# Combine weights transposed four token tiles at a time, and the output product on four groups of 32 rows in three passes

## The chip, the cores and the metric

The kernel runs on one core of a Trainium2 chip. Its five engines are TensorE (matmuls, with weight loads as instructions of their own), VectorE, ScalarE, GpSimd and SyncE, which here only issues transfers. The metric is the device time of one execution in microseconds; lower is better.

## What is computed

Three stages in float32: a linear attention with a normalisation over the head dimension, a feed-forward layer with the gate h * cos(h), and a soft mixture of experts. The change lies in the last one. There are 4608 tokens of 512 channels, 8 experts with 4 slots each (32 slots), and a hidden size of 1024 per expert.

```python
logits = x @ phi                                  # 4608 x 32
d = exp(logits - logits.max(0)); d /= d.sum(0) + 1e-9
slot_input = (d.T @ x).reshape(8, 4, 512)
for e in range(8):
    slot_out[e] = maximum(slot_input[e] @ w1[e], 0) @ w2[e]
c = exp(logits - logits.max(1)); c /= c.sum(1) + 1e-9
out = c @ slot_out.reshape(32, 512)               # 4608 x 512
```

The last line is the output product: for each token the 32 combine weights `c` times the 32 slot outputs.

## The kernel before

**Body.** The tokens go through in ten blocks (eight of 512 tokens, two of 256). For each block the first matrix of the feed-forward layer is applied in 16 column groups (`main`, line 389, three matmuls in place of one, because each operand is split in a high and a low part of the reduced type fp32r), the cosine gate runs on ScalarE and VectorE, and logits and slot inputs are accumulated. Steps for the next block (attention, loads, transposes) are woven into this loop at slots given by the table PLAN; each engine runs its own instructions in the order in which they are written down, since the schedule is manual. The body ends near 610 us.

**Tail.** `tail` (line 743) holds everything that the change touches but a small setup. The 32 slots are handled as two sets G of four experts. `first_layer(G)` and `relu(G)` make the hidden activations, `h_T` transposes them, `second_layer(G, h)` (line 795) multiplies with the second matrix for one half h of the 512 channels. It has eight steps r; in a step four matmuls write to four groups of 32 output partitions, one for each expert, and each float32 matmul is two instructions. Its argument `then` names other work to be put behind a step r on TensorE. Its result is copied to `so[G]` by ScalarE (line 805).

**Combine weights.** `c_softmax` leaves the weights as `tok[0]`, 128 tokens by 36 tiles by 32 slots. The output product needs them transposed, slots on partitions, and split in a high and a low part. `c_split(j)` (line 716) makes, on GpSimd, for four token tiles the three blocks high, low, high of 32 columns each; `c_T(j)` (line 727) transposes each of these four 96-column tiles with a matmul against the identity, and ScalarE or VectorE copies the 512 columns out of PSUM (line 736). There are nine j, so 36 transposes.

**Output product.** `select(h)` (line 807) gathers the 32 slot rows of a half from the two `so` by a matmul with a constant 0/1 matrix `sel`, three copies of them on 96 partitions: high, high and low part. `part_out(h, u)` (line 818) then makes output tile u (six for each half: three token groups n by two blocks k of 128 channels): three matmuls of 96 rows by 512 tokens, so that high*high, high*low and low*high are summed within one matmul. Each result is copied from PSUM to `ot` by VectorE or ScalarE in turn, and SyncE writes the 768 KB tile out (line 831; the very last tile in three pieces, line 829).

**Banks.** PSUM has the pools `ps_m` (three banks, tags "h"), `ps_l` (one) and `ps_a` (four, through `at_bank`). `part_out` uses the three of `ps_m`.

**Loads.** The expert matrices are read by `fill`, in order of use, into any buffer that has come free, on the queue of SyncE. The lists `early`, `mid` and `last` (lines 1029 to 1032) are issued within the tail; an issue waits until the former content of its buffer was read, and everything behind it on that queue waits too. `sel_init` (line 1035) builds the selection matrix on GpSimd during block 3.

Of the kernel before, what the change touches and what calls it, by code (L numbers as in the profile page):

```python
# [8 lines left out]
F32 = mybir.dt.float32  # L9
F32R = mybir.dt.float32r  # L10
I32 = mybir.dt.int32
AF = mybir.ActivationFunctionType
ALU = mybir.AluOpType
# [20 lines left out]
    start=(  # L34
# [3 lines left out]
    ),  # L38
# [18 lines left out]
    lo=(1, 1, 0, 0),  # L57
# [5 lines left out]
TB = 512  # L63
# [4 lines left out]
NT = sum(TT)  # L68
# [4 lines left out]
def tile_linear_attention__ffn_cos__soft_moe(  # L73
# [14 lines left out]
    nc = tc.nc  # L88
    B, H, D = kv.shape[0], 8, 64
    NF, KD = w_in.shape[0], w_in.shape[2]  # L90
    NS = phi.shape[2]

    const = ctx.enter_context(tc.tile_pool(name="const", bufs=1))
    w_p = ctx.enter_context(tc.tile_pool(name="w", bufs=1))
    x_p = ctx.enter_context(tc.tile_pool(name="x", bufs=1))
# [8 lines left out]
    one_p = ctx.enter_context(tc.tile_pool(name="one", bufs=1))  # L104
    ps_m = ctx.enter_context(tc.tile_pool(name="ps_m", bufs=PLAN["pm"], space=bass.MemoryType.PSUM))
    ps_l = ctx.enter_context(tc.tile_pool(name="ps_l", bufs=1, space=bass.MemoryType.PSUM))
    ps_a = ctx.enter_context(tc.tile_pool(name="ps_a", bufs=PLAN["pa"], space=bass.MemoryType.PSUM))

    ident = const.tile([128, 128], F32, name="ident")
    rep32 = const.tile([128, NS], F32, name="rep32")  # L110
    rep = const.tile([128, 4, NS], F32, name="rep")
    sel = const.tile([128, 2, 3, NS], F32, name="sel")
    mhalf = const.tile([128, H], F32, name="mhalf")
    hpi = const.tile([128, 1], F32, name="hpi")
    gn = const.tile([128, 1], F32, name="gn")
    phi_sb = const.tile([128, KD, NS], F32, name="phi_sb")
# [14 lines left out]
    tok = []  # L131

    def at_bank(name):
        return ps_a.tile([128, 512], F32, tag="at", name=name)

    def copy_on(e, out, in_):
        (nc.vector.tensor_copy if e else nc.scalar.copy)(out=out, in_=in_)
# [573 lines left out]
        nc.vector.reciprocal(out=st[:, 1], in_=st[:, 1])  # L711
        nc.vector.tensor_tensor(out=l_tok, in0=l_tok, in1=st[:, 1].to_broadcast([128, n, NS]), op=ALU.mult)

    cs_t, cT_t = [], []

    def c_split(j):
        if j == 0:
            w = x_p.tile([128, 9, 4, 3 * NS], F32, tag="x1", name="cs")
            cs_t.extend(w[:, x] for x in range(9))
        cs = cs_t[j]  # L720
        c = tok[0][:, 4 * j:4 * j + 4, :]
        hi, lo, hi2 = (cs[:, :, i * NS:(i + 1) * NS] for i in range(3))
        nc.gpsimd.tensor_copy(out=hi.bitcast(F32R), in_=c)
        nc.gpsimd.tensor_tensor(out=lo.bitcast(F32R), in0=c, in1=hi, op=ALU.subtract)
        nc.gpsimd.tensor_copy(out=hi2.bitcast(F32R), in_=c)

    def c_T(j):
        if j % 4 == 0:
            n = min(9 - j, 4)
            pool, tag = ((x_p, "x00"), (x_p, "x01"), (w_p, "w9"))[j // 4]  # L730
            x = pool.tile([128, n, 512], F32R, tag=tag, name="cT")
            cT_t.extend(x[:, i] for i in range(n))
        ps = at_bank("cT")
        for t in range(4):
            nc.tensor.transpose(ps[0:96, t * 128:(t + 1) * 128], cs_t[j][:, t, :], ident)
        copy_on(j % 2 == 0, cT_t[j][0:96], ps[0:96])

    def warm(n):
        ps = at_bank("warm")
# [3 lines left out]
    def tail():  # L743
        nc.vector.tensor_scalar(out=s_run, in0=s_run, scalar1=1e-9, scalar2=None, op0=ALU.add)
        nc.vector.reciprocal(out=s_run, in_=s_run)
        ps = si_t.pop()
# [4 lines left out]
        for i in range(2):  # L751
            cc = slice(128 * i, 128 * i + 128)
            nc.vector.tensor_scalar(out=flat[:, cc], in0=ps[:, cc], scalar1=s_run, scalar2=None, op0=ALU.mult)
            cc = slice(128 * i + 256, 128 * i + 384)
# [3 lines left out]
        ps = at_bank("sT").rearrange("p (k s) -> p k s", s=128)  # L758
        for kk in (0, 2, 1, 3):
            nc.tensor.matmul(out=ps[:, kk, 0:NS], lhsT=part[:, kk], rhs=rep32, start=True, stop=True)  # L760
        for G in range(2):
            nc.vector.tensor_copy(out=Z[G][:, :, :, 0:4],
                                  in_=ps[:, :, 16 * G:16 * G + 16].rearrange("p k (i t) -> p k i t", t=4))
# [26 lines left out]
            (nc.scalar.copy if u else nc.vector.tensor_copy)(out=dst, in_=ps)  # L790

        so = [a_p.tile([128, 512], F32, tag="a", name="so") for _ in range(2)]
        st_all = one_p.tile([128, 2, 256], F32R, tag="ls", name="st")

        def second_layer(G, h, then={}):
            ps = (at_bank("eo") if h == 2 else ps_m.tile([128, 512], F32, tag="h", name="eo"))[:, 0:256]
            c = (h - 1) * 256
            for r in range(8):
                for i in range(4):
                    w = GR.pop((4 * G + i, 1, h, r))  # L800
                    nc.tensor.matmul(out=ps[32 * i:32 * i + 32, :], lhsT=hT[G][0][:, r, 32 * i:32 * i + 32],  # L801
                                     rhs=w, start=(r == 0), stop=(r == 7))
                for fn, *a in then.get(r, ()):
                    fn(*a)
            nc.scalar.copy(out=so[G][:, c:c + 256], in_=ps)

        def select(h):
            cc = slice(256 * (h - 1), 256 * h)
            ps = at_bank("sel")[:, 0:256]
            for G in range(2):  # L810
                nc.tensor.matmul(out=ps[0:96], lhsT=sel[:, G].rearrange("p c s -> p (c s)"), rhs=so[G][:, cc],
                                 start=(G == 0), stop=(G == 1))
            st = st_all[:, h - 1]
            nc.scalar.activation(out=st[0:96], in_=ps[0:96], func=AF.Copy)
            nc.vector.tensor_tensor(out=st[64:96], in0=ps[64:96], in1=st[64:96].bitcast(F32), op=ALU.subtract)
            return st

        def part_out(h, u):
            st, ots = half[h]
            ot = ots[u]  # L820
            n, k = divmod(u, 2)
            for v in range(3):
                ps = ps_m.tile([128, 512], F32, tag="h", name="fo")
                nc.tensor.matmul(out=ps, lhsT=st[0:96, 128 * k:128 * k + 128], rhs=cT_t[3 * n + v][0:96],  # L824
                                 start=True, stop=True)
                cc = slice(512 * v, 512 * v + 512)
                copy_on((3 * u + v) % 2, ot[:, cc], ps)
                if (h, u) == (2, 5):
                    nc.sync.dma_start(out=out[3, 2, :, cc], in_=ot[:, cc])
            if (h, u) != (2, 5):  # L830
                nc.sync.dma_start(out=out[2 * h - 2 + k, n], in_=ot)

        def two(pool, tag):
            t = pool.tile([128, 2, 1536], F32, tag=tag, name="ot")
            return [t[:, 0], t[:, 1]]
# [6 lines left out]
        relu(1)  # L842
        for fn, *args in mid:
            fn(*args)
        for j in range(9):
            c_split(j)
        second_layer(0, 1, {2: [(h_T, 1, 0)], 4: [(h_T, 1, 1)], 6: [(c_T, 0)]})
        for fn, *args in last:
            fn(*args)
        assert not todo  # L850
        second_layer(1, 1, {0: [(c_T, 1)], 4: [(c_T, 2)]})
        half = {}

        def first_half():
            half[1] = (select(1), two(g_p, "g1") + [gt_p.tile([128, 1536], F32, tag=f"gt{i}", name="ot") for i in (1, 0)]
                       + two(g_p, "g0"))

        second_layer(0, 2, {0: [(first_half,)], 1: [(c_T, 3)], 2: [(part_out, 1, 0)], 4: [(part_out, 1, 1)],
                            5: [(c_T, 4)], 6: [(c_T, 5)]})
        second_layer(1, 2, {0: [(part_out, 1, 2)], 2: [(part_out, 1, 3)], 3: [(c_T, 6)], 4: [(c_T, 7)], 5: [(c_T, 8)],  # L860
                            7: [(part_out, 1, 4)]})
        half[2] = (select(2), [t_p.tile([128, 1536], F32, tag="T2", name="ot")] + two(g_p, "g1")
                   + [gt_p.tile([128, 1536], F32, tag="gt1", name="ot")] + two(g_p, "g0"))
        part_out(1, 5)
# [95 lines left out]
    for b in range(1, B):  # L960
        p, i = divmod(b, 2)
        n, sl = b - 2, PLAN["kv"]
        if b < 4:
            n, sl = PLAN["K"][b - 1]
# [3 lines left out]
    for j in range(1, NB):  # L968
        n = min(j - 1, SMALL - 1)
# [5 lines left out]
        for t in range(TT[j]):  # L975
            i = T0[j] + t + 3
# [25 lines left out]
    for u in range(NF):  # L1002
        n, i = 3 + u // 4, u % 4
        a, f = PLAN["nt"][i]
# [22 lines left out]
    for n in range(8, 15):  # L1027
        ld_at(9, max(n + 1, 10), fill, w_p, f"w{n}", 2)
    early = [(fill_kv, i) for i in range(4)] + [(fill, rem_p, "vr", 1), (fill, rem_p, "kr", 2), (fill, t_p, "T2", 4)] + [
        (fill, q_p, f"q{i}", 1) for i in range(3)] + [(fill, const, "kvA", 2)]  # L1030
    mid = [(fill, w_p, f"w{n}", 2) for n in range(10, 13)]
    last = [(fill, w_p, f"w{n}", 2) for n in range(13, 16)]
    Z = []

    def sel_init():
        nc.gpsimd.memset(sel, 0.0)
        id4 = ident.rearrange("p (i t) -> p i t", t=32)[:, :, 0:4]
        for G in range(2):
            for c in range(3):
                nc.gpsimd.tensor_copy(  # L1040
                    out=sel[:, G, c, 16 * G:16 * G + 16].rearrange("p (i t) -> p i t", t=4), in_=id4)

    late(3, 2, sel_init)

    def z_init():
# [44 lines left out]
    with tc.manual_schedule():  # L1090
# [34 lines left out]
        for j, f in [(j, f) for j in range(SMALL, NB) for f in range(0, NF, 2)]:  # L1125
            if (j, f) == (NB - 1, NF - 2):
                for i in range(2):
                    ps = ps_m.tile([128, 512], F32, tag="h", name="h")[:, 0:256]
# [10 lines left out]
            ps = ps_m.tile([128, 512], F32, tag="h", name="h")  # L1139
# [22 lines left out]
        fill(t_p, "T1", 4)  # L1162
        fill(t_p, "T0", 4)
        tail()
        assert not any((side, post, fin, loads))

# [55 lines left out]
```

## Time and profile before

| | |
|---|---|
| time, median of 3 runs | 685.14 us (684.58 to 687.48) |
| the profiled execution | 686.2 us, of which its span is 684.2 us |
| TensorE matmuls busy | 659.3 us, 96% of the span |
| VectorE, ScalarE, GpSimd busy | 497.9, 332.4, 217.4 us (73%, 49%, 32%) |
| granted TensorE clock, mean | 0.987 of full speed |
| read and written over the span | 91.29 MB and 13.63 MB |

The span runs from the first instruction of the profiled execution to its last; the time of the execution holds 2.0 us more around it. A share of busy time is a mean over the whole span, and the tail's 75 us are a ninth of it, so the rows below are nearly all from the tail.

### The profile page before, as it was taken

The page shows a single profiled execution, that of the slowest core. Times are in us where ns is not written, and L with a number is a line of the kernel's source. Part 1 is how long each engine was busy: PE and PEld are TensorE (multiplying, and loading weights), DVE is VectorE, ACT ScalarE, POOL GpSimd, SP SyncE. Part 2 cuts the span into 40 slices and gives each one's busy share as a digit, 9 for nine tenths or more (in the row PEclk, how much of TensorE's full clock was granted, in tenths as well). Part 3 has the DMA queues.
Part 4 walks back from the last instruction along what each step waited for, and adds up shares of the span by engine and source line. Part 5 has one row for each costly group of instructions (what it writes and reads, how often), then busy time and mean ns, then how long its engine had stood idle before and what let it go on. Part 6 is the DMA issues. An engine that isn't in the chain of part 4 may idle for free.

```text
span 684.2 us, 12526 instructions
## 1 busy us (share of the span) xinstructions
PE 659.3 (96%) x4580; PEld 479.3 (70%) x4580; DVE 497.9 (73%) x895; ACT 332.4 (49%) x589; POOL 217.4 (32%) x320
## 2 busy tenths in 40 slices
PE   7989999999999999999999999999999999999994
PEld 6767877776667776776777677767767779863542
DVE  3899989966677778887887888778877756444143
ACT  3576767645345445436455444544545344641243
POOL 3351111320364434521633344154335423002200
PEclk9999999999999999999999999999999999999995
DMA  9944564111374627783767378486534498999968
GB/s 334 350 167 175 181 217 167 60 34 62 92 187 139 185 63 219 210 212 111 192 191 192 106 200 233 102 226 175 131 105 96 84 319 249 362 394 408 399 247 322
DMA packets 72892, 135.11 MB, mean 197 GB/s; under 512 B 11008, under 2 KB 38784, under 8 KB 72448
## 3 DMA queue, kind: packets, MB, share of 16 engines
q1 hardware_dynamic: 65664, 119.63, 53.9%
q0 software_dynamic: 7168, 14.69, 9.2%
q8 instruction: 36, 0.59, 0.3%
q14 instruction: 24, 0.20, 0.1%
HBM read 91.29 MB, written 13.63 MB: 153 GB/s over the span
## 4 chain that ended last, share of the span: by engine, by line
PE 68%; DVE 12%; ACT 6%; SPq 5%; DMA 5%; issue 3%; POOL 0%; DVEq 0%; ACTq 0%
PE h L389 39%; PE ab L622 5%; SPq L511 4%; PE ops L202 3%; DMA g<-tr 3%; PE l L523 3%; PE eo L801 2%; DVE gT L451 2%; PE eh L771 2%; DVE tmp L408 2%; PE fo L824 2%; PE tr L492 2%; PE xTps L239 2%; ACT tmp L412 2%; PE kvps L183 2%
## 5 line engine op out<-in xcount | busy, mean ns | idle before, releaser
L389 PE MATMUL h<-xt,w 128*128 128x512 f32 (+1 forms) x1920 | 421.0, 374 | 4.1 <-DVE xt L252 1.7
L389 PEld LDWEIGHTS h<-xt,w 128*128 128x128 f32 x1920 | 329.5, 189 | 87.1 <-issue 12.7
L412 ACT ACTIVATE tmp<-tmp,hpi 128x512 f32<-128x512 f32 (+1 forms) x145 | 104.3, 721 | 173.4 <-DVE tmp L408 173.2
L511 POOL DMA_DIRECT2D g<-tr x224 | 123.8, 555 | 101.1 <-DVE tr L470 49.0
L451 DVE TENSOR_TENSOR gT<-tmp,h 128x512 f32<-128x512 f32 x130 | 89.2, 686 | 70.6 <-ACT tmp L412 70.5
L214 POOL TENSOR_TENSOR ri<-ss,mhalf 128x8 f32<-128x8 f32 x36 | 59.7, 1662 | 202.1 <-DVE ss L212 197.2
L408 DVE SCALAR_TENSOR_TENSOR tmp<-h,tmp 128x512 f32<-128x512 f32 (+1 forms) x145 | 97.1, 673 | 21.0 <-ACT tmp L405 20.2
L405 ACT ACTIVATE tmp<-h 128x512 int32<-128x512 f32 (+1 forms) x145 | 85.3, 588 | 48.4 <-PE h L389 48.1
L470 DVE STREAM_TRANSPOSE tr<-gT 128x512 f32<-128x512 f32 x103 | 73.2, 711 | 5.9 <-DMA g<-tr 1.5
L325 POOL TENSOR_TENSOR w<-st_m,w 128x512 fp32r<-128x512 f32 x16 | 21.4, 1340 | 68.6 <-ACT w L320 65.3
L202 PE MATMUL ops<-kvA,q 128*128 128x128 f32 (+1 forms) x320 | 38.3, 278 | 0.1
L243 ACT ACTIVATE xt<-xTps,gn 128x512 fp32r<-128x512 f32 x36 | 24.3, 684 | 27.4 <-PE xTps L239 27.4
L202 PEld LDWEIGHTS ops<-kvA,q 128*128 128x128 f32 (+1 forms) x320 | 34.4, 180 | 3.2 <-issue 2.3
L622 PE MATMUL ab<-g,d 128*32 128x512 f32 x256 | 32.3, 593 | 0.0
L523 PE MATMUL l<-gT,wp 128*32 128x512 f32 (+1 forms) x248 | 30.9, 556 | 0.0
L209 ACT ACTIVATE sq<-ops 128x512 f32<-128x512 f32 x32 | 19.1, 596 | 22.0 <-PE ops L202 21.8
L252 DVE SCALAR_TENSOR_TENSOR xt<-xTps,gn,xt 128x512 fp32r<-128x512 f32 x36 | 26.1, 730 | 4.9 <-ACT xt L243 4.6
L211 DVE TENSOR_REDUCE ss<-sq 128x8 f32<-128x512 f32 x32 | 21.6, 676 | 7.1 <-ACT sq L209 6.7
L183 PEld LDWEIGHTS kvps<-kv 128*64 128x64 f32 x448 | 15.4, 137 | 11.6 <-issue 7.6
L239 PE MATMUL xTps<-ident,sq 128*128 128x128 f32 x128 | 19.7, 277 | 3.4 <-DVE sq L221 3.4
L622 PEld LDWEIGHTS ab<-g,d 128*32 128x32 f32 x256 | 9.4, 110 | 19.3 <-issue 16.8
L221 DVE TENSOR_TENSOR sq<-ops,ri 128x512 f32<-128x512 f32 x32 | 21.5, 676 | 1.2 <-POOL ri L214 1.2
(185 smaller groups left out, 634.9 us busy)
## 6 DMA issues: line engine op xcount, KB each, us to landing
kv<-in_kv SPq DMA_DIRECT2D x28, 512.0 KB, 5.4
g<-tr SPq DMA_DIRECT2D x224, 64.0 KB, 3.6
g<-tr POOLq DMA_DIRECT2D x224, 64.0 KB, 3.7
ew<-in_w2h SPq DMA_DIRECT2D x19, 512.0 KB, 10.0
q<-in_qT SPq DMA_DIRECT2D x36, 256.0 KB, 5.9
out<-ot SPq DMA_DIRECT2D x11, 768.0 KB, 4.4
rw<-in_w_in SPq DMA_DIRECT2D x16, 512.0 KB, 4.6
nat<-in_w_out SPq DMA_DIRECT2D x16, 512.0 KB, 4.0
```

Of the source, the lines that this page charges most:

```text
L202: nc.tensor.matmul(out=ps[p0:p0 + n, pr * 128:(pr + 1) * 128], lhsT=q_t[j, t][:, pr, p0:p0 + n], rhs=kvbd[b % 2][:, pr, :], start=True, st ...
L214: nc.gpsimd.tensor_tensor(out=ri[:, :, 0], in0=ss, in1=mhalf, op=ALU.pow)
L239: nc.tensor.transpose(ps[:, kk * 128:(kk + 1) * 128], xs[:, kk * 128:(kk + 1) * 128], ident)
L389: nc.tensor.matmul(out=ps, lhsT=w[:, a, kk, :], rhs=x[b][:, kk, :], start=(n == 0), stop=(n == 3 * KD - 1))
L405: nc.scalar.activation(out=t.bitcast(I32), in_=ps, func=AF.Copy, bias=0.25, scale=INV_2PI)
L408: nc.vector.scalar_tensor_tensor(out=t, in0=ps, scalar=INV_2PI, in1=t.bitcast(I32), op0=ALU.mult, op1=ALU.subtract)
L412: nc.scalar.activation(out=t, in_=t, func=AF.Sin, bias=hpi, scale=TWO_PI)
L451: nc.vector.tensor_tensor(out=g, in0=fr, in1=h_t.pop((j, f)), op=ALU.mult)
L470: nc.vector.transpose(out=tr_t[j, q][:, :, i, :], in_=gT_t[j, n * q + i].rearrange("p (b t) -> p b t", t=32))
L511: (nc.gpsimd if b % 2 else nc.sync).dma_start(out=dst[32 * b:32 * b + 32, :, x, a:a + n, :].rearrange("p t f i -> p t (f i)"), in_=src[32 ...
L523: nc.tensor.matmul(out=l_t[j][32 * o:32 * o + 32, :], lhsT=wp[:, f, :], rhs=gT_t.pop((j, f)), start=(c == 0), stop=(c == (2 if j == NB - 1 ...
L622: nc.tensor.matmul(out=ps[32 * c:32 * c + 32, :], lhsT=d[:, t, :], rhs=gs[c // 2][t][:, (c % 2) * 512:(c % 2) * 512 + 512], start=(t == 0) ...
```

## The change

1. `c_split` goes. `c_T(n)` (three calls) transposes four token tiles of 32 slots at once, 128 columns by 128 tokens, three such transposes into one bank of 384 columns. ScalarE copies the bank as the high part, VectorE subtracts to get the low part. Slot s of tile 4i + g then lies on partition 32g + s. Nine transposes stand in place of 36, all behind step 6 of `second_layer(0, 1)`.
2. `select` makes four copies of the 32 rows on 128 partitions, with two matrices `sel` and `phi_sb` (the buffer of phi, which is free by then). ScalarE copies the high part, VectorE subtracts for the low part, all 128 partitions each.
3. `part_out` uses the four groups of 32 partitions as four separate products of 384 tokens: three passes (high*high, high*low, low*high), each of four matmuls into four banks. Four copies of 384 columns empty them. The three odd tiles of the second half use the four banks of `ps_a`, the others those of `ps_m` and `ps_l`. The last tile goes out in four pieces.
4. The transposed weights lie in the buffer x1 in place of x00, x01 and w9, so the last loads go to w9 and x00 in place of w13 to w15. The places at which the first half's output tiles are woven into `second_layer` move.
5. The host reorders the output by the new token order.

```diff
-    sel = const.tile([128, 2, 3, NS], F32, name="sel")
+    sel = const.tile([128, 4, NS], F32, name="sel")
-    def c_split(j):
...
-        hi, lo, hi2 = (cs[:, :, i * NS:(i + 1) * NS] for i in range(3))
-        nc.gpsimd.tensor_copy(out=hi.bitcast(F32R), in_=c)
-        nc.gpsimd.tensor_tensor(out=lo.bitcast(F32R), in0=c, in1=hi, op=ALU.subtract)
-        nc.gpsimd.tensor_copy(out=hi2.bitcast(F32R), in_=c)
-    def c_T(j):
...
-        ps = at_bank("cT")
-        for t in range(4):
-            nc.tensor.transpose(ps[0:96, t * 128:(t + 1) * 128], cs_t[j][:, t, :], ident)
-        copy_on(j % 2 == 0, cT_t[j][0:96], ps[0:96])
+    def c_T(n):
+        if not cT_t:
+            x = x_p.tile([128, 4096], F32R, tag="x1", name="cT")
+            m = NT * NS
+            cT_t.extend(x[:, m * i:m * i + m] for i in range(2))
+            cT_t.append(x[:, 2 * m:2 * m + 1024].rearrange("p (h a c) -> p h a c", h=2, a=2))
+        ps = at_bank("cT")[:, 0:384]
+        for t in range(3):
+            i = 4 * (3 * n + t)
+            nc.tensor.transpose(ps[:, t * 128:(t + 1) * 128], tok[0][:, i:i + 4, :].rearrange("p t s -> p (t s)"), ident)
+        hi, lo = (x[:, 384 * n:384 * n + 384] for x in cT_t[0:2])
+        nc.scalar.copy(out=hi, in_=ps)
+        nc.vector.tensor_tensor(out=lo, in0=ps, in1=hi.bitcast(F32), op=ALU.subtract)
...
         def select(h):
-            for G in range(2):
-                nc.tensor.matmul(out=ps[0:96], lhsT=sel[:, G].rearrange("p c s -> p (c s)"), rhs=so[G][:, cc],
+            for G, t in enumerate((sel, phi_sb)):
+                nc.tensor.matmul(out=ps, lhsT=t.rearrange("p c s -> p (c s)"), rhs=so[G][:, cc],
...
-            nc.scalar.activation(out=st[0:96], in_=ps[0:96], func=AF.Copy)
-            nc.vector.tensor_tensor(out=st[64:96], in0=ps[64:96], in1=st[64:96].bitcast(F32), op=ALU.subtract)
+            hi, lo = (cT_t[2][:, h - 1, a] for a in range(2))
+            nc.scalar.copy(out=hi, in_=ps)
+            nc.vector.tensor_tensor(out=lo, in0=ps, in1=hi.bitcast(F32), op=ALU.subtract)
         def part_out(h, u):
-            for v in range(3):
-                ps = ps_m.tile([128, 512], F32, tag="h", name="fo")
-                nc.tensor.matmul(out=ps, lhsT=st[0:96, 128 * k:128 * k + 128], rhs=cT_t[3 * n + v][0:96],
-                                 start=True, stop=True)
-                cc = slice(512 * v, 512 * v + 512)
-                copy_on((3 * u + v) % 2, ot[:, cc], ps)
+            if h == 2 and u % 2:
+                ps = [at_bank("fo") for _ in range(4)]
+            else:
+                ps = [ps_m.tile([128, 512], F32, tag="h", name="fo") for _ in range(3)]
+                ps.append(ps_l.tile([128, TB], F32, tag="l", name="fo"))
+            for p, (a, b) in enumerate(((0, 0), (0, 1), (1, 0))):
+                for i in range(4):
+                    r = slice(32 * i, 32 * i + 32)
+                    nc.tensor.matmul(out=ps[i][:, 0:384], lhsT=st[a][r, 128 * k:128 * k + 128],
+                                     rhs=cT_t[b][r, 384 * n:384 * n + 384], start=(p == 0), stop=(p == 2))
+            for i in range(4):
+                cc = slice(384 * i, 384 * i + 384)
+                copy_on(i % 2, ot[:, cc], ps[i][:, 0:384])
...
-        second_layer(0, 1, {2: [(h_T, 1, 0)], 4: [(h_T, 1, 1)], 6: [(c_T, 0)]})
-        second_layer(1, 1, {0: [(c_T, 1)], 4: [(c_T, 2)]})
+        second_layer(0, 1, {2: [(h_T, 1, 0)], 4: [(h_T, 1, 1)], 6: [(c_T, n) for n in range(3)]})
+        second_layer(1, 1)
-        second_layer(0, 2, {0: [(first_half,)], 1: [(c_T, 3)], 2: [(part_out, 1, 0)], 4: [(part_out, 1, 1)],
-                            5: [(c_T, 4)], 6: [(c_T, 5)]})
-        second_layer(1, 2, {0: [(part_out, 1, 2)], 2: [(part_out, 1, 3)], 3: [(c_T, 6)], 4: [(c_T, 7)], 5: [(c_T, 8)],
-                            7: [(part_out, 1, 4)]})
+        second_layer(0, 2, {1: [(first_half,)], 3: [(part_out, 1, 0)], 5: [(part_out, 1, 1)], 7: [(part_out, 1, 2)]})
+        second_layer(1, 2, {2: [(part_out, 1, 3)], 5: [(part_out, 1, 4)]})
...
-    mid = [(fill, w_p, f"w{n}", 2) for n in range(10, 13)]
-    last = [(fill, w_p, f"w{n}", 2) for n in range(13, 16)]
+    mid = [(fill, w_p, f"w{n}", 2) for n in range(9, 13)] + [(fill, x_p, "x00", 4)]
     def sel_init():
-        nc.gpsimd.memset(sel, 0.0)
         id4 = ident.rearrange("p (i t) -> p i t", t=32)[:, :, 0:4]
-        for G in range(2):
-            for c in range(3):
-                nc.gpsimd.tensor_copy(
-                    out=sel[:, G, c, 16 * G:16 * G + 16].rearrange("p (i t) -> p i t", t=4), in_=id4)
+        for G, t in enumerate((sel, phi_sb)):
+            nc.gpsimd.memset(t, 0.0)
+            for c in range(4):
+                nc.gpsimd.tensor_copy(out=t[:, c, 16 * G:16 * G + 16].rearrange("p (i t) -> p i t", t=4), in_=id4)
```

## Rows read from the trace of the kernel before

**Rows 1.** Busy time by stretch: length; PE, PEld, DVE, ACT, POOL; clock, DMA share, GB/s.

```profile
646.00:650.00 4.00, 4.00 (x42) 1.99 (x35) 0.42 (x1) 1.33 (x3) 0.00 (x0) 1.00 1.01 404
662.00:664.00 2.00, 2.00 (x21) 1.07 (x13) 1.02 (x2) 0.70 (x2) 0.00 (x0) 1.00 0.00 0
669.00:682.00 13.00, 6.52 (x13) 3.50 (x13) 5.01 (x8) 4.00 (x7) 0.00 (x0) 0.51 1.01 403
682.00:684.20 2.20, 0.00 (x0) 0.00 (x0) 0.00 (x0) 0.00 (x0) 0.00 (x0) 0.50 0.02 7
```

**Rows 2.** Timeline of SyncE's queue: start, length of issue, line, transfer, count.

```profile
642.99 0.33 SPq L682 DMA_DIRECT2D ew<-in_w2h  x1
...
667.63 1.55 SPq L831 DMA_DIRECT2D out<-ot  x2
...
675.32 3.79 SPq L829 DMA_DIRECT2D out<-ot  x3
```

**Rows 3.** Chain that ended last, in order: start, us, what, instructions.

```profile
590.22 0.44 PE tr L492 x4
...
618.70 0.83 PE sT L760 x8
...
635.77 1.29 PE eo L801 x24
637.07 0.64 PE hT L788 x4
...
640.35 0.57 PE cT L735 x4
...
646.80 1.03 PE sel L811 x4
...
648.97 0.57 PE eo L801 x8
649.54 0.90 PE fo L824 x3
...
662.84 0.45 PE fo L824
663.30 1.07 ACT ot L137 x2
664.38 0.29 ACT so L805
...
664.71 0.67 PE sel L811 x2
```

**Rows 4.** Groups by line and shape from 610 us: busy us, mean ns, idle before.

```profile
L137 DVE COPY ot<-fo 128x512 f32<-128x512 f32 x18 | 12.2, 690 | 9.1 <-PE fo L824 9.0
L137 ACT COPY ot<-fo 128x512 f32<-128x512 f32 x18 | 10.3, 587 | 9.0 <-PE fo L824 8.9
L805 ACT COPY so<-eo 128x256 f32<-128x256 f32 x4 | 1.5, 378 | 4.9 <-PE eo L801 4.9
L815 DVE TENSOR_TENSOR st<-sel,st 32x256 fp32r<-32x256 f32 x2 | 0.8, 422 | 4.2 <-ACT st L814 4.2
```

**Rows 5.** Timeline of GpSimd: start, us, line, instruction, idle before and releaser.

```profile
629.04 0.29 POOL L723 CAST cs<-l_tok 128x128 fp32r<-128x128 f32 x1 [10.92 <-DVE l_tok L712]
...
637.92 0.29 POOL L725 CAST cs<-l_tok 128x128 fp32r<-128x128 f32 x1
...
246.94 1.67 POOL L214 TENSOR_TENSOR ri<-ss,mhalf 128x8 f32<-128x8 f32 x1 [4.96 <-DVE ss L212]
...
248.89 0.88 POOL L1040 COPY sel<-ident 128x16 f32<-128x16 f32 x6
```

**Rows 6.** Weight loads of 96, 128 and 32 rows, view of rows 4.

```profile
L824 PEld LDWEIGHTS fo<-cT,st 96*128 96x128 f32 x36 | 7.5, 220 | 7.3 <-ACT ot L137 3.2 <-DVE ot L137 2.2 <-issue 0.8
L741 PEld LDWEIGHTS warm<-ident 128*128 128x128 f32 x10 | 1.2, 191 | 0.8 <-issue 0.8
L608 PEld LDWEIGHTS lrT<-ident,we 32*128 32x128 f32 x2 | 0.2, 134 | 0.8 <-issue 0.8
```

More of the change, by code (lines that the diff above doesn't have):

```diff
@@ L712, in c_softmax @@
         nc.vector.tensor_tensor(out=l_tok, in0=l_tok, in1=st[:, 1].to_broadcast([128, n, NS]), op=ALU.mult)
-    cs_t, cT_t = [], []
-    def c_split(j):
[L717 to L721, printed above, removed]
-        hi, lo, hi2 = (cs[:, :, i * NS:(i + 1) * NS] for i in range(3))
-        nc.gpsimd.tensor_copy(out=hi.bitcast(F32R), in_=c)
-        nc.gpsimd.tensor_tensor(out=lo.bitcast(F32R), in0=c, in1=hi, op=ALU.subtract)
-        nc.gpsimd.tensor_copy(out=hi2.bitcast(F32R), in_=c)
-    def c_T(j):
[L728 to L732, printed above, removed]
-        ps = at_bank("cT")
-        for t in range(4):
-            nc.tensor.transpose(ps[0:96, t * 128:(t + 1) * 128], cs_t[j][:, t, :], ident)
-        copy_on(j % 2 == 0, cT_t[j][0:96], ps[0:96])
+    cT_t = []
+    def c_T(n):
[11 more added lines that the diff above has]
+        nc.vector.tensor_tensor(out=lo, in0=ps, in1=hi.bitcast(F32), op=ALU.subtract)
     def warm(n):
@@ L792, in tail @@
         so = [a_p.tile([128, 512], F32, tag="a", name="so") for _ in range(2)]
-        st_all = one_p.tile([128, 2, 256], F32R, tag="ls", name="st")
         def second_layer(G, h, then={}):
@@ L809, in select @@
             ps = at_bank("sel")[:, 0:256]
-            for G in range(2):
-                nc.tensor.matmul(out=ps[0:96], lhsT=sel[:, G].rearrange("p c s -> p (c s)"), rhs=so[G][:, cc],
+            for G, t in enumerate((sel, phi_sb)):
+                nc.tensor.matmul(out=ps, lhsT=t.rearrange("p c s -> p (c s)"), rhs=so[G][:, cc],
                                  start=(G == 0), stop=(G == 1))
-            st = st_all[:, h - 1]
-            nc.scalar.activation(out=st[0:96], in_=ps[0:96], func=AF.Copy)
-            nc.vector.tensor_tensor(out=st[64:96], in0=ps[64:96], in1=st[64:96].bitcast(F32), op=ALU.subtract)
-            return st
+            hi, lo = (cT_t[2][:, h - 1, a] for a in range(2))
+            nc.scalar.copy(out=hi, in_=ps)
+            nc.vector.tensor_tensor(out=lo, in0=ps, in1=hi.bitcast(F32), op=ALU.subtract)
+            return hi, lo
         def part_out(h, u):
@@ L844, in tail @@
             fn(*args)
-        for j in range(9):
-            c_split(j)
-        second_layer(0, 1, {2: [(h_T, 1, 0)], 4: [(h_T, 1, 1)], 6: [(c_T, 0)]})
-        for fn, *args in last:
-            fn(*args)
         assert not todo
-        second_layer(1, 1, {0: [(c_T, 1)], 4: [(c_T, 2)]})
+        second_layer(0, 1, {2: [(h_T, 1, 0)], 4: [(h_T, 1, 1)], 6: [(c_T, n) for n in range(3)]})
+        second_layer(1, 1)
         half = {}
@@ L1215 @@
     r = run_bass_kernel_spmd(nc, [arrays], core_ids=[0])
-    o = r.results[0]["out_0"].transpose(1, 3, 0, 2).reshape(4, 1152, 512)
+    o = r.results[0]["out_0"].reshape(4, 3, 128, 4, 3, 128).transpose(1, 4, 3, 5, 0, 2).reshape(4, 1152, 512)
     got = np.empty((4, 2, 576, 512), o.dtype)
```

## The prediction

> **What bounds the kernel now.** I read the page first: TensorE is busy 96% of the span, and in its clock row only the last of 40 slices is low, so the body is TensorE-bound and the change doesn't touch it. Everything that it touches lies after 629 us, apart from a small setup at 249 us. So I read the busy time by stretch next, and there the limit changes twice [rows 1]. Until 650 us the DMA engines are full (404 GB/s, weights), and TensorE too. From 650 to 664 TensorE is busy without a gap while DMA falls to 0.00 between single output tiles (the row from 662): here TensorE's own list of work decides. From 669 to 682 DMA is at 1.01 and 403 GB/s, TensorE at half, its clock at 0.50: here the output writes decide. The issues of the SyncE queue [rows 2] show what these writes are: one 768 KB tile for each (half, group), the sixth issued at 667.63 in the pair of that row, then the full tiles of the second half, from 675.32 on its last tile in three pieces. The sixth and the six of the second half are 7 x 0.786 = 5.5 MB; at 403 to 406 GB/s that is 13.6 us, which is the full stretch (about 668.5 to 682.05). So the end stands **16.57 us after the issue of (half 1, group 5)** (684.2 - 667.63), and whatever moves that issue moves the end by as much, as long as the later tiles keep up with 1.94 us each.
>
> What sets 667.63 is in the chain of waits [rows 3]: second-layer matmuls ("eo"), 4-transpose pieces ("cT") and output triples ("fo") on TensorE without a gap up to 662.84, then an evacuation on ScalarE (1.07), the copy "so", the selection (0.67), the last triple.
>
> **Part by part.** Prices on TensorE, from the chain [rows 3]: 24 and 8 eo instructions took 1.29 and 0.57 us. 8 instructions are one step r (4 matmuls in two instructions each), so a run of k steps costs about 0.14 + 0.43k (the long run, which follows other work of the same kind, has no 0.14), the 0.14 being the switch from other work. A cT piece takes 0.57, a triple of outputs 0.90, the selection 1.03. Four 128x128 transposes take 0.44 without a switch, 0.64 with one ("hT"): 0.11 each and 0.20 for the switch.
>
> *Transposes.* Nine pieces of 0.57 (5.13 us) go; nine 128x128 transposes in one run come, 0.20 + 9 x 0.11 = 1.19. Minus 3.9 us, all before 662.84. With them go switches: from 640.35 to 662.84 the eo steps (25 of them) run in 14 pieces, afterwards in 7: minus 7 x 0.14 = 1.0 us.
>
> *Splitting.* 27 GpSimd instructions go; they lie beside TensorE work from 629 to 638.2 [rows 5] and their first reader starts at 640.35 [rows 3], so nothing is gained. The split moves to three ScalarE copies and three VectorE subtractions of 384 columns. By the copies of 256 and 512 [rows 4] that is 0.48 and 0.56 us each, 1.5 us on either engine after 641, where ScalarE's next work is the "so" copy at about 642.3, needed only at 646.4. Nothing on the path.
>
> *Output product.* For one group, three matmuls of 96 rows and 512 columns become twelve of 32 rows and 384 columns, four at a time in different row groups. Call the new piece X. The present triple advances by 0.22 a matmul, so 384 columns take 0.165; three passes that run four at once take 0.50, with the switch X = 0.70. Above that stands the weight load: 12 in place of 3. The eight sT matmuls move only 32 columns, so their 0.83 us [rows 3] is nearly all weight load: 0.104 each; 12 of them one behind the other give 1.25 + 0.20 = 1.45. Between 0.70 and 1.45 I take **0.90**, since the triple of today is the nearest row (same number type, its weight loads included). No row shows several row groups at once. The nearest are the four column groups of eo: a step of 8 instructions of 256 columns advances in 0.43 us, while the four ungrouped ones of the selection, of 256 columns too, need 1.03 [rows 3], which would be 2.1 for 8. So four column groups do run at once.
> The Trainium skill, "TensorE: Matmul & The Clock Gate", section "Measured speedup vs the span model", gives 3.07 times for four row groups of 32; by that, as an estimate, X would be 0.20 + 12 x 0.165 / 3.07 = 0.85. No run here shows it yet.
>
> *Selection.* 128 columns of weights for 96: 1.05 for 1.03. ScalarE and VectorE take 0.38 and 0.42 as now (256 columns).
>
> *Evacuation.* Three copies of 512 become two ScalarE copies of 384 (0.96) and two VectorE ones (1.11), but all four banks end in the last pass, so a tile is out some 1.2 us after its matmuls. In the first half each group uses the same four banks, and two groups are 1.0 us apart (two eo steps): some 0.15 us of stall, twice, 0.3 in all (0 to 0.6).
>
> *Loads.* The last weight loads (w13 to w15) become w9 and x00; bytes and order stay. w9 is free when the first layer ends (635.77 [rows 3]), and its place in the queue comes up at about 637 (the last six loads of 512 KB take 1.3 us each, and the last is issued at 642.99 [rows 2]). DMA is full of weights to about 650; the last second layer would begin at 658.8 - 3.86 (8 steps) - 1.8 (two pieces) = 653.1. Nothing gained or lost; the cover is 3 us.
>
> *Setup.* sel_init becomes 2 memsets and 8 copies for 1 and 6: +0.25 + 2 x 0.2 = 0.65 us of GpSimd at 249 us. GpSimd had idled 4.96 us before its last step there and has nothing after it until 255 (the last two of [rows 5]): zero (0 to 0.65).
>
> **The sum.** From 640.35: 1.19, 25 steps at 0.43 in 7 runs (11.73), selection 1.05, five output pieces. The last eo step ends at 654.32 + 5X = 658.8, with stalls 659.1 (now 662.84; there it had four pieces ahead of it, now five). Piece 4 was done two steps earlier, so ScalarE ends its copies at about 659.1 and "so" at 659.55 (now 664.66: a second gain, of 1.4). Selection to 660.3, piece 5 to 661.2, copies 1.2: issue at **662.4**, 5.2 us earlier. Before it, five tiles of 1.94 us from about 651 on leave DMA free by 662. Tile (2,0) follows: banks free at 662.3, matmuls to 662.9, copies to 664.1, issued at 664.1, 1.7 after (1,5): just in time for 1.94. After that a group needs 1.1 on VectorE and 0.9 on TensorE; even at half clock X is near 1.8. So DMA decides again, and 662.4 + 16.57 = 679.0 for the span in place of 684.2. The profiled run took 686.2 (2.0 around the span), and would take 681.0; the median of the runs is 685.14, 1.06 below it, so the forecast is 685.14 - 5.2 = **679.9 us**.
>
> Bounds within this case: X = 0.70 and no stall gives 678.2; a four-piece last tile in place of three, with shorter rows, 0 to +0.4; transposes at 0.16 each +0.5. About 677.5 to 681.5.
>
> **Rivals.**
> (A) *The row groups don't run at once.* Then X is 0.20 + 12 x 0.165 = 2.2, up to 2.8 with half of a weight load of 0.104 before each. From X = 1.94 on TensorE paces the last stage instead of DMA, and the span becomes 654.32 + 5X, plus 1.5 for copy and selection, plus 7X for the last seven pieces, plus some 4.8 for bank wait, last copies, issue, last piece and end: 660.6 + 12X. That passes 684.2 at X = 1.97; at 2.2 the time is 688, at 2.8 it is 695. I take 691, slower. For: no row shows row groups at once; the kernel's own narrow products are all column groups. Against: the four column groups do.
> (B) *Twelve weight loads decide*, at X = 1.45: the last eo step at 661.6, issue of (1,5) at 665.5, the span 682.1, time 683, within 0.5%. The rows speak half against it: the load of 32 rows lasts 134 ns where that of 96 lasts 220 and that of 128 191 [rows 6], and eo hides its loads.
> The Trainium skill, same page, section "LDWEIGHTS (loading the stationary operand)", speaks for B: a 32x128 load takes as long as a 128x128 one, 128 / 1.2 = 107 ns; by that estimate X is 0.20 + 12 x 0.107 = 1.48 where nothing hides it. The durations here differ with the rows, so the trace doesn't agree as far as a duration tells.
> (C) *It does not reach the end*: TensorE gets to the last second layer before its weights are there, or a copy in the wrong place holds (1,5). It needs the load stream to slip by over 3 us. Time 683 to 685.
>
> **How the numbers follow.** Forecast 0.70, A 0.14, B 0.12, C 0.04. A measurement of this kernel tells about 0.5% (3.4 us) from no change. Faster by that is below 681.7: the forecast but its upper end, 0.67. Slower is above 688.6: A but its lower end, with something for a half-clock last stage under B, 0.13. The rest, 0.20, within. The range goes from 677.5 over B and C to 685.5, and leaves out A and the tails.
>
> **What would show it.** Right: nine transposes in about 1.2 us near 640.4; twelve output matmuls starting in fours within some 0.02 us, a piece of 0.7 to 1.0; "so" of the last half at about 659.5; the sixth output issue near 662.4; DMA full from there to the end. Wrong: starts of output matmuls spaced by 0.16 (A) or weight loads spaced by 0.1 (B), a low DMA share in the last stretch, eo steps that wait for a load. The forecast would be most wrong in X, which counts six times ahead of the issue.

## The result, and the profile after

The changed kernel takes **679.78 us** (679.31 to 680.11, four runs), the kernel before 684.86 in the same comparison: ratio 0.9918, 95% interval 0.9892 to 0.9944. The forecast was 679.9. The profiled execution took 680.11, its span 678.3 in place of 684.2.

Busy time by stretch of the kernel after, in the columns of [rows 1]:

```profile
650.00:662.40 12.40, 11.83 (x175) 6.70 (x171) 6.17 (x14) 5.86 (x16) 0.00 (x0) 1.00 0.90 364
662.00:664.00 2.00, 2.00 (x35) 1.70 (x29) 1.60 (x4) 1.63 (x4) 0.00 (x0) 1.00 0.81 318
662.40:675.50 13.10, 4.64 (x61) 3.64 (x53) 5.75 (x12) 4.94 (x12) 0.00 (x0) 0.84 1.00 402
```

The kernel before, from the end of the weight loads to its last stretch:

```profile
650.00:669.00 19.00, 17.79 (x151) 8.45 (x149) 9.63 (x15) 8.45 (x17) 0.00 (x0) 1.00 0.58 236
```

The stretch in which TensorE alone decided, with DMA partly idle, is nearly gone. From 650 us to the last stretch DMA is at 0.90 over 12.4 us, where it was at 0.58 over 19; from 662 to 664 it is at 0.81, where [rows 1] has 0.00. The full last stretch, 669 to 682 in [rows 1], now runs from 662.4 to 675.5. It is as long as before (13.1 us shown, 402 GB/s) and starts about 6 us earlier.

The issues of SyncE's queue (compare [rows 2]) and the chain (compare [rows 3]) after:

```profile
661.71 2.20 SPq L829 DMA_DIRECT2D out<-ot  x2
```

```profile
640.81 1.13 PE cT L725 x9
641.94 4.89 PE eo L792 x88
646.83 1.06 PE sel L802 x4
647.89 1.00 PE eo L792 x16
648.89 0.73 PE fo L821 x11
...
650.62 0.92 PE fo L821 x10
...
656.91 0.73 PE fo L821 x12
657.64 1.00 PE eo L792 x16
658.64 1.19 PE sel L802 x4
659.83 0.77 PE fo L821 x8
```

Nine transposes in one run take 1.13 us; behind them 11 steps run on in one piece (4.89). The pair of issues shown holds output tile (half 1, group 5), (1,5) for short, at 661.71 for 667.63, and the end follows it by 16.59 us (678.3 - 661.71), as it followed by 16.57. (A count below 12 in an output piece is a gap in the records.)

### The profile page after: what moved, and what is told of

Read it like the earlier page. It is cut to its first block, busy times and chain, and to the rows that moved or that the text cites. A ratio compares the mean times of both kernels' runs of the same rounds, so it can differ in the third digit from the quotient of the medians.

```text
span 678.3 us, 12659 instructions
## 1 busy us (share of the span) xinstructions
PE 649.5 (96%) x4661; PEld 476.3 (70%) x4661; DVE 495.3 (73%) x899; ACT 331.2 (49%) x594; POOL 208.9 (31%) x296
## 4 chain that ended last, share of the span: by engine, by line
PE 69%; DVE 12%; DMA 6%; ACT 6%; issue 3%; SPq 2%; POOL 1%; DVEq 0%; ACTq 0%
PE h L389 42%; PE ab L622 4%; PE ops L202 4%; PE l L523 3%; DMA g<-tr 3%; PE eo L792 2%; PE eh L763 2%; DVE gT L451 2%; PE kvps L183 2%; ACT tmp L412 2%; DVE tmp L408 2%; PE tr L492 2%; PE xTps L239 2%; PE l L532 2%; DVE tr L470 1%
## 5 line engine op out<-in xcount | busy, mean ns | idle before, releaser
L325 POOL TENSOR_TENSOR w<-st_m,w 128x512 fp32r<-128x512 f32 x16 | 21.4, 1338 | 67.8 <-ACT w L320 67.8
L221 DVE TENSOR_TENSOR sq<-ops,ri 128x512 f32<-128x512 f32 x32 | 21.4, 675 | 1.2 <-POOL ri L214 1.2
```

## The experiments

Executions differ by up to 2.7 us in where the body ends and the tail begins, so the profiles below are compared by three distances: from the start of the first transposes of the combine weights ("cT") to the issue of output tile (1,5), from there to the end, and their sum. Times and ratios are against the kernel before in the same comparison.

| kernel | cT start | issue of (1,5) | end | cT to issue | issue to end | sum | ratio (95%) |
|---|---|---|---|---|---|---|---|
| before | 640.35 | 667.63 | 684.2 | 27.28 | 16.57 | 43.85 | 1 |
| after | 640.81 | 661.71 | 678.3 | 20.90 | 16.59 | 37.49 | 0.9918 (0.9892 to 0.9944) |
| 36 transposes | 639.79 | 665.69 | 682.2 | 25.90 | 16.51 | 42.41 | 0.9981 (0.997 to 0.9991) |
| before, 9 transposes | 640.15 | 662.28 | 678.9 | 22.13 | 16.62 | 38.75 | 0.9924 (0.9912 to 0.9937) |
| half writes | 641.82 | 662.72 | 674.7 | 20.90 | 11.98 | 32.88 | 0.9848 (0.9833 to 0.9862) |
| group by group | 639.99 | 660.95 | 677.5 | 20.96 | 16.55 | 37.51 | 0.9904 (0.9892 to 0.9917) |
| one row group | 640.05 | 669.71 | 694.5 | 29.66 | 24.79 | 54.45 | 1.017 (1.0154 to 1.0187) |
| one bank set | 641.31 | 662.21 | 679.5 | 20.90 | 17.29 | 38.19 | 0.9921 (0.9908 to 0.9933) |
| piece 4 last | 639.15 | 660.62 | 677.2 | 21.47 | 16.58 | 38.05 | 0.9919 (0.9905 to 0.9933) |
| earlier issue | 641.21 | 660.90 | 677.9 | 19.69 | 17.0 | 36.69 | 0.9903 (0.9888 to 0.9918) |
| after, again | 640.16 | 661.06 | 677.7 | 20.90 | 16.64 | 37.54 | 0.99 (0.9885 to 0.9914) |
| earlier issue, again | 639.33 | 659.02 | 677.0 | 19.69 | 17.98 | 37.67 | 0.9889 (0.9872 to 0.9905) |

**The 27 transposes put back on TensorE.**

```diff
+    def pad_T():
+        ps = at_bank("pT")
+        for t in range(3):
+            nc.tensor.transpose(ps[:, t * 128:(t + 1) * 128], tok[0][:, 4 * t:4 * t + 4, :].rearrange("p t s -> p (t s)"), ident)
-        second_layer(0, 1, {2: [(h_T, 1, 0)], 4: [(h_T, 1, 1)], 6: [(c_T, n) for n in range(3)]})
-        second_layer(1, 1)
+        second_layer(0, 1, {2: [(h_T, 1, 0)], 4: [(h_T, 1, 1)], 6: [(c_T, n) for n in range(3)] + [(pad_T,)]})
+        second_layer(1, 1, {0: [(pad_T,)], 4: [(pad_T,)]})
...
```

(six more `pad_T`, behind steps 2, 4 and 6 of the first and 1, 3 and 6 of the last second layer)

> The changed kernel with 27 more transposes on TensorE, three each behind nine second-layer steps, near the places of the old ones; nothing reads them. Theory T (the gain is the transposes and switches that TensorE no longer has ahead of the issue of (half 1, group 5), and the end follows that issue by 16.6 us): TensorE has 27 x 0.11 and up to 8 more switches of 0.14 to 0.26 ahead of that issue, 4.1 to 5.1 us; the issue goes from 661.7 to about 666, the time from 679.8 to 684 to 685, as before the change. Rival P (the product on four row groups brings the gain): time stays at 680 to 681, since the product is untouched.

Measured 684.76 us, the kernel before 686.09 in the same comparison. The chain of this kernel shows what a piece of three costs among the steps, and its queue when tile (1,5) was issued:

```profile
640.92 0.33 PE pT L733 x3
641.25 1.00 PE eo L797 x16
642.25 0.48 PE pT L733 x3
```

```profile
665.69 0.33 SPq L834 DMA_DIRECT2D out<-ot  x1
```

The issue comes 5.0 us later (25.90 for 20.90), the end still 16.51 behind it. Most of the gain is given back, though the new output product is in place: theory T, and against P. The tail stays 1.4 us shorter than before (42.41 for 43.85).

**Nine transposes in the kernel before.**

```diff
-        ps = at_bank("cT")
-        for t in range(4):
-            nc.tensor.transpose(ps[0:96, t * 128:(t + 1) * 128], cs_t[j][:, t, :], ident)
-        copy_on(j % 2 == 0, cT_t[j][0:96], ps[0:96])
+        if j % 3 == 0:
+            nine.append(at_bank("cT"))
+        ps = nine[-1][0:96, (j % 3) * 128:(j % 3) * 128 + 128]
+        nc.tensor.transpose(ps, cs_t[j][:, 0, :], ident)
...
-        second_layer(0, 1, {2: [(h_T, 1, 0)], 4: [(h_T, 1, 1)], 6: [(c_T, 0)]})
+        second_layer(0, 1, {2: [(h_T, 1, 0)], 4: [(h_T, 1, 1)], 6: [(c_T, j) for j in range(9)]})
```

(the other `c_T` calls go; three at a time are copied, each to all four places of its tile)

> The kernel before with only nine of its 36 transposes, in one run behind step 6 of the second layer; each transposed tile is copied to all four places (so three quarters of the combine weights are those of another tile). Output product, selection and loads stay those of before. Theory T: TensorE loses 5.13 - 1.15 us of transposes and eight switches of 0.14, so the last second-layer step ends at 657.7 in place of 662.8; the issue of (1,5) comes 5 us earlier, time 679.5 to 680.5, the whole gain without the new product. Rival P (the product brings it): 683.5 to 685.

Measured 680.75 us. Chain and issue of that kernel:

```profile
640.15 1.12 PE cT L736 x9
641.27 4.45 PE eo L806 x80
...
655.19 2.30 PE eo L806 x40
657.49 0.44 PE fo L829
```

```profile
662.28 0.33 SPq L836 DMA_DIRECT2D out<-ot  x1
```

The last step ends at 657.49 (657.7 was worked out), and of the 6.4 us by which the tail shortens from before to after (43.85 - 37.49), 5.1 are there with the old output product. The other 1.3 us are what product, copies and order of pieces bring together, in agreement with the 1.4 of the experiment before; the ratios, 0.9924 and 0.9918, don't tell the two kernels apart.

**Half of the output of five tiles.**

```diff
             if (h, u) != (2, 5):
-                nc.sync.dma_start(out=out[2 * h - 2 + k, n], in_=ot)
+                w = slice(0, 768 if h == 2 else 1536)
+                nc.sync.dma_start(out=out[2 * h - 2 + k, n][:, w], in_=ot[:, w])
```

(the other half of these five tiles stays unwritten)

> The changed kernel with the first five output tiles of the second half written to half their columns only (the rest of those rows of the output stays unwritten). Theory T (the last 14 us are the output writes): 5 x 0.39 MB less, 4.8 us of transfer at 403 GB/s; the end is then set by the last copies (about 668.5) and the last tile's transfer, span 673 to 674.5, time 674.5 to 676. Rival (copies out of PSUM and TensorE at half clock set the end): time stays at 679 to 680.

Measured 675.61 us. Busy time by stretch, columns as in [rows 1]:

```profile
668.00:670.00 2.00, 0.06 (x1) 0.00 (x0) 1.48 (x4) 0.79 (x3) 0.00 (x0) 1.00 1.01 393
670.00:672.00 2.00, 0.00 (x0) 0.00 (x0) 0.00 (x0) 0.00 (x0) 0.00 (x0) 0.66 1.02 382
```

The tail is 4.6 us shorter for 4.8 us of transfers left out, with no other edit: output writes set the end, and neither copies nor TensorE's clock.

**Two orders of the twelve matmuls.** First the loops exchanged:

```diff
-            for p, (a, b) in enumerate(((0, 0), (0, 1), (1, 0))):
-                for i in range(4):
+            for i in range(4):
+                for p, (a, b) in enumerate(((0, 0), (0, 1), (1, 0))):
```

> The changed kernel with the two loops of the output product exchanged: all three passes of one row group, then the next group; the same 48 weight loads and matmuls for each four pieces, but matmuls of one row group stand behind one another. Theory T with four groups at once in the changed kernel: the piece goes from 0.73 to between 0.20 + 9 x 0.165 = 1.7 and 0.20 + 12 x 0.165 = 2.2 us, the issue of (1,5) 5 to 7 us later less 0.5 for copies that start earlier, time 684 to 687, more (to 691) if the clock falls in the last stage. If row groups never ran at once, or if the piece's length is of no matter: 680, as the changed kernel.

Measured 679.4 us, as the changed kernel, where 684 to 687 was expected. The chain, and the busy time of the tile "fo" alone in two slices of the first piece (length; PE, PEld, DVE, ACT; clock, DMA share, GB/s):

```profile
648.07 0.75 PE fo L821 x12
```

```profile
648.00:648.20 0.20, 0.20 (x4) 0.20 (x8) 0.00 (x0) 0.00 (x0) 1.00 0.97 389
648.20:648.40 0.20, 0.20 (x8) 0.20 (x10) 0.00 (x0) 0.00 (x0) 1.00 0.98 389
```

The piece is as long as in the other order, and four matmuls are under way in the first slice, although the first three written down belong to one row group. So that run could not tell the theories apart: it did not make the groups run one by one. That needed them to share one row group:

```diff
-                    r = slice(32 * i, 32 * i + 32)
+                    r = slice(0, 32)
```

> The changed kernel with all four products of a piece on row group 0 (operands of partitions 0 to 31 for all, so three quarters of the tokens get the weights of another tile); instructions, sizes and waits stay. The exchange of loops before this left the piece at 0.75 us, since TensorE went on with the next row group while the first was taken; on one row group that is not possible. Theory T with rival A's piece: 0.20 + 12 x 0.165 = 2.2 us or more, last second-layer step 7 us later than 658.6, issue of (1,5) at about 670, and from there TensorE paces the last stage: time 687 to 695. If the number of row groups in use is of no matter: 680.

Measured 697.49 us, slower than before by 1.7%. Its chain, one slice of "fo" alone, and two stretches later on, the second over all 72 matmuls of the last six pieces:

```profile
648.13 2.30 PE fo L821 x12
...
668.99 21.40 PE fo L821 x72
```

```profile
648.40:648.60 0.20, 0.20 (x3) 0.20 (x2) 0.00 (x0) 0.00 (x0) 1.00 1.08 430
```

```profile
672.00:674.00 2.00, 2.00 (x8) 2.00 (x7) 0.24 (x1) 0.00 (x0) 0.00 (x0) 0.50 0.67 270
669.00:690.40 21.40, 21.37 (x72) 20.63 (x72) 6.60 (x13) 5.80 (x13) 0.00 (x0) 0.57 0.54 221
```

The same twelve instructions take 2.30 us in place of 0.73, so four row groups do run at once in the changed kernel (2.30 / 0.73 = 3.2). Matmuls and weight loads are both busy throughout (0.20 of 0.20 us), so this run doesn't tell which of the two paces a piece on one row group. This is rival A made real: issue 8.8 us later, then 72 matmuls in 21.4 us on TensorE with DMA at 0.54. It goes 2.5 us above the expected range, since the granted clock fell to 0.50 within that stage (0.57 on average) and a piece grew from 2.3 to 3.6 us on average (21.4 / 6).

**One set of banks in the second half.**

```diff
-            if h == 2 and u % 2:
+            if False:
```

> The changed kernel with all pieces of the second half on the same four PSUM banks (no second set for the odd tiles). Theory T (transfers pace the last stage at 1.94 us a tile): a piece and its copies in series take 0.75 + 1.2 = 2.0 us, about as long as a tile's transfer, so 0 to +0.8 us: 679.5 to 680.8. Rival E (copies out of PSUM pace the last stage and the second set hides them): each of the last five pieces waits for all copies of the one before, 0.9 us more each, 683 to 685.

Measured 680.17 us. The pieces of TensorE one after the other, and busy time in two stretches, columns as in [rows 1]:

```profile
661.62 1.37 PE L821 MATMUL fo<-cT 32*128 32x384 f32 x12 [0.55 <-ACT ot L137]
663.39 1.90 PE L821 MATMUL fo<-cT 32*128 32x384 f32 x12 [0.41 <-ACT ot L137]
665.59 1.86 PE L821 MATMUL fo<-cT 32*128 32x384 f32 x12 [0.30 <-ACT ot L137]
667.71 1.90 PE L821 MATMUL fo<-cT 32*128 32x384 f32 x12 [0.26 <-ACT ot L137]
```

```profile
663.00:664.00 1.00, 0.61 (x6) 0.53 (x7) 0.91 (x2) 0.72 (x2) 0.00 (x0) 0.89 1.02 406
664.00:677.00 13.00, 9.20 (x58) 6.21 (x58) 5.11 (x10) 4.30 (x10) 0.00 (x0) 0.50 0.92 367
```

Pieces and copies now alternate, about 2.16 us a piece (667.71 - 663.39 for two). That is a little over a tile's transfer of 1.94, and the tail is 0.7 us longer. But the clock plays a part: here it falls to 0.50 within the slice from 663, while TensorE still works, in the changed kernel only behind its work. The one round before that, from 661.62 to 663.39, takes 1.77 us, less than a transfer. What the second set would be worth at full clock isn't shown. Rival E's price of 0.9 us for each piece isn't there: as long as a tile takes the copies and TensorE no longer than the writes, their waits are covered.

**Piece 4 behind the last step.**

```diff
-        second_layer(1, 2, {2: [(part_out, 1, 3)], 5: [(part_out, 1, 4)]})
+        second_layer(1, 2, {2: [(part_out, 1, 3)], 7: [(part_out, 1, 4)]})
```

> The changed kernel with output piece (half 1, group 4) behind step 7 of the last second layer, as in the kernel before, in place of step 5. Theory T as predicted (the copy of the last second-layer result stood behind that piece's two copies on ScalarE): the last step ends 0.9 us earlier, the copy 'so' 0.8 us later (659.1 to 659.9), the issue of (1,5) 0.8 us later, time +0.6 to +1.0. If ScalarE's order is of no matter: 0 or slightly below.

Measured 680.77 us; the interval doesn't tell it from the changed kernel. The chain does:

```profile
656.11 0.76 PE fo L821 x8
656.88 0.85 ACT ot L137 x2
657.72 0.29 ACT so L796
```

The copy "so" ends 1.9 us behind the last step (656.11 to 658.01), 1.5 us more than the 0.44 of the changed kernel. The last step itself ends 0.9 us earlier (16.96 us behind the start of cT for 17.83), and the issue of (1,5) is 0.57 us later in sum; 0.8 was expected.

**An earlier issue.** The selection one step earlier, pieces (1,0) to (1,4) one step earlier each, (1,5) ahead of the second selection, tile (2,0) in two halves:

```diff
+        part_out(1, 5)
         half[2] = (select(2), [t_p.tile([128, 1536], F32, tag="T2", name="ot")] + two(g_p, "g1")
                    + [gt_p.tile([128, 1536], F32, tag="gt1", name="ot")] + two(g_p, "g0"))
-        part_out(1, 5)
...
+                elif (h, u) == (2, 0) and i % 2:
+                    cc = slice(768 * (i // 2), 768 * (i // 2) + 768)
+                    nc.sync.dma_start(out=out[2, 0, :, cc], in_=ot[:, cc])
```

> The changed kernel with the selection one step earlier (behind step 0), pieces (1,0) to (1,4) one step earlier each, piece (1,5) ahead of the second selection, and tile (2,0) written in two halves. Theory T (after the weights, at 650, only the gaps of the transfer stream are left: 0.4 us at 650 to 652 and 1.0 us at 661 to 663): the issue of (1,5) comes at about 660.3 in place of 661.7 and the stream has no gap, time 0.6 to 1.2 us below the changed kernel. If the order costs as much elsewhere: no difference.

> The changed kernel once more, on the same chip as the version with the earlier issue, for a direct comparison: ratio to the kernel before 0.991 to 0.993; end 16.6 us after the issue of (1,5).

> The version with the earlier issue once more, beside the changed kernel. Theory T: 0.6 to 1.2 us below it (0.1 to 0.2%), from the two gaps of the transfer stream that it closes; the last stage of output transfers without a slice below 0.9. If the order costs as much elsewhere: the same time.

First comparison: 679.46 us, ratio 0.9903 (0.9888 to 0.9918). Second, side by side: 678.8, ratio 0.9889 (0.9872 to 0.9905), against 679.58, 0.99 (0.9885 to 0.9914), for the changed kernel. The medians differ by 0.8 us as expected, but the intervals overlap, so a gain isn't shown. Stretches of the second comparison, the changed kernel and then this version:

```profile
661.00:662.00 1.00, 1.00 (x22) 0.98 (x22) 0.25 (x1) 0.28 (x1) 0.00 (x0) 1.00 0.61 244
```

```profile
652.00:660.00 8.00, 7.54 (x116) 4.17 (x112) 3.94 (x8) 3.85 (x10) 0.00 (x0) 1.00 1.01 418
661.00:662.00 1.00, 1.00 (x14) 0.90 (x14) 1.00 (x3) 0.96 (x3) 0.00 (x0) 1.00 1.04 413
662.00:663.00 1.00, 1.00 (x19) 0.82 (x13) 1.00 (x3) 0.86 (x2) 0.00 (x0) 1.00 0.93 381
```

The gap in the transfer stream (0.61) is closed to a slice of 0.93. The issue of (1,5) comes 1.2 us earlier behind the start of cT (19.69 for 20.90), but the end stands 17.0 and 17.98 us behind it, not 16.6: the tail is 0.8 us shorter than that of the changed kernel in the first execution, and no shorter in the second (37.67 for 37.54). So here the end no longer follows the issue, but the stream of transfers ahead of it. With the stream this full, only fewer bytes or an earlier start of the loads should shorten the tail further; that wasn't tried.

## Why the prediction came out

**What bounds the tail: right, up to a limit.** The end follows the issue of (1,5) by 16.5 to 16.6 us in six kernels whose issue lies between 660.62 and 667.63. Cutting the writes shortens that distance (11.98). It grows where a piece takes longer than a tile's 1.94 us of transfer (2.16 with its copies: 17.29; 2.3 and more: 24.79), and also where the issue comes so early that the transfers ahead of it leave no gap (17.0 and 17.98 with the earlier issue). The prediction's "whatever moves that issue moves the end by as much" lacks this second condition; the changed kernel lies just short of it.

**Transposes: right.** 1.13 us for 1.19, one run for nine pieces, and alone worth 5.1 us of tail, where the prediction's terms give 3.9 and 1.0. The saved switches are part of it.

**Output product: the mechanism was right, the size off.** The row groups run at once, rival A is out. X was the mis-sized term: 0.73 where nothing waits, not 0.90. Of its bounds it lies next to the lower one, 0.70, so the present triple was the wrong row to take: twelve weight loads add almost nothing, since they don't follow one another (144 loads of 183 ns take 7.9 us in all). The first four matmuls of a piece start within 0.02 us, the sign that the prediction named; first "fo" alone in a slice of that length, then groups by line and shape of the kernel after (compare [rows 4, 6]):

```profile
648.81:648.83 0.02, 0.01 (x4) 0.01 (x4) 0.00 (x0) 0.00 (x0) 1.00 1.04 410
```

```profile
L821 PE MATMUL fo<-cT 32*128 32x384 f32 x144 | 11.0, 373 | 0.6 <-ACT ot L137 0.6
L821 PEld LDWEIGHTS fo<-cT 32*128 32x128 f32 x144 | 7.9, 183 | 4.1 <-ACT ot L137 2.3 <-issue 0.7 <-ACT so L796 0.4
L137 DVE COPY ot<-fo 128x384 f32<-128x384 f32 x24 | 11.9, 549 | 5.9 <-PE fo L821 5.6 <-issue 0.3
L137 ACT COPY ot<-fo 128x384 f32<-128x384 f32 x24 | 10.1, 485 | 7.4 <-PE fo L821 7.1
```

Rival B, twelve loads in a row, is out by the same 0.73. But my argument against it from the durations was a poor one. The 220 of [rows 6] is a mean that holds loads at half clock; the loads of 96 rows at full clock, in the kernel before:

```profile
L824 PEld LDWEIGHTS fo<-cT,st x12: 186/188/189, 649.5 to 657.8; 96*128 96x128 f32 x12
```

A load of 32 rows lasts 183 ns here, not the 134 of the f32 one in [rows 6]. So the load time of this type hardly shrinks with the rows. The Trainium skill, "TensorE: Matmul & The Clock Gate", section "LDWEIGHTS (loading the stationary operand)", says that it goes by the columns and not by the rows; with 183 ns for 32 rows and 188 for 96 the trace agrees as to the rows, but not with its 107 ns for 128 columns. My estimate X = 1.48 from that figure, for loads that nothing hides, did not come about.
The gain of 3.07 that the Trainium skill, same page, section "Measured speedup vs the span model", gives for four row groups stands beside 2.30 / 0.73 = 3.2 here. My estimate from it, X = 0.85, was nearer than the 0.90 that I took.

**Copies, stalls, selection: right.** 0.485 and 0.549 us a copy for 0.48 and 0.56; the selection 1.06 for 1.05; one stall of 0.19 (a piece of 0.92) and one of 0.04 for 0.3 in all.

**The second gain: right.** "so" ends 0.44 us behind the last step (1.82 before), 1.4 us sooner as predicted:

```profile
658.71 0.37 ACT L796 COPY so<-eo 128x256 f32<-128x256 f32 x1 [0.19 <-PE eo L792]
```

It is not 1.4 us for nothing, since the fifth piece ahead of the last step delays that step by 0.9. Undoing the move alone costs 0.57 us.

**How the sum closed.** From cT to the issue I had 22.05 us (662.4 - 640.35), measured 20.90: 1.15 less, six times 0.17 from X. Against that the body of the profiled execution ended 0.46 us later, so the span is 678.3 for 679.0. That the median differs from the forecast by only 0.1 us is luck: the profiled execution came out 0.9 us below its forecast (680.11 for 681.0), and the median lies only 0.33 below it, where the prediction carried over 1.06 from the kernel before. The lower bound of the prediction was off in its sum too: X = 0.70 and no stall take 6 x 0.20 + 0.3 off 679.9, which is 678.4, not 678.2.

**Loads, splitting, setup: nothing that a row shows.** From 640 to 668 TensorE waits only once after the change, for a copy of an output tile:

```profile
PE fo L821 <- ACT ot L137: 0.6, 1, 0.6
```

So rival C is out. The 0.46 us in the body can't be told from the spread between executions; in kernels with the same setup cT starts between 639.15 and 641.82.

## What to carry to other kernels

Look for the event behind which the rest of the kernel has a fixed length (here the sixth output issue, 16.6 us ahead of the end), and price a change by what it takes off the work ahead of that event, as long as the transfers before it leave gaps. Behind the event, longer work of the engines costs nothing until it takes more than the transfers that pace it. Small matmul pieces strewn among others cost a switch on each side besides themselves, so packing 36 transposes into nine and running them in one go brought 5.1 of the 6.4 us of tail; the times of the two kernels don't show the rest. An experiment meant to make things serial has to be read in the trace before its time is believed: the exchange of loops changed nothing on the engine.

## What the runs showed of the hardware

- TensorE did not keep to the written order across row groups, against what is said above of every engine. Written group by group, the twelve matmuls of a piece still ran four at a time and took 0.75 us; on one row group the same twelve took 2.30.
- The granted clock fell from 1.00 to 0.50 at about 672 in the kernel with one row group, while TensorE's rows were busy for the whole of each stretch; since about 669 it had run nothing but 32-row matmuls on one row group, without other work between. With four row groups at once, the clock was still 1.00 at the end of TensorE's work in the changed kernel (667). It fell near 663.8 in the kernel with one set of banks, where TensorE, on four row groups too, had waited for copies ahead of the pieces at 661.62 and 663.39 (0.55 and 0.41 us).
- A weight load of 32 rows in fp32r lasts 183 ns at full clock, that of 96 rows 186 to 189. Loads of four row groups overlap: twelve of them fit into a piece of 0.73 us.
